# A fused attention and mixture-of-experts kernel on one core: first loads of the second stage issued some slots sooner, and four more weight pieces converted in its first pass

## The chip, the cores and the metric

The kernel runs on one core of a Trainium2 chip. The core has five engines that run programs of their own and wait for each other by semaphores: PE (TensorE, matmuls), DVE (VectorE), ACT (ScalarE), POOL (GpSimd) and SP (SyncE, here the queue that issues most DMAs; ACT issues a few). The time is device microseconds (us) of one execution; the kernel before has a median of 885.64 us over three.

## The reference

Three blocks stand behind each other. The weights `moe_w_in` and `moe_w_out` come as 8-byte floats, everything else as 4-byte ones.

```python
# 1: attention that mixes its heads before and after the softmax (4 x 12 heads x 448 x 64)
scores = scale * np.matmul(q, k.transpose(0, 1, 3, 2))
scores = np.einsum('bhij,hg->bgij', scores, w_pre)
attn = softmax(scores)
attn = np.einsum('bhij,hg->bgij', attn, w_post)
x = np.matmul(attn, v)                 # as 1792 tokens x 768
# 2: a gated layer, 768 -> 2048 -> 768
h = x @ w_in
x = (h - np.tanh(h)) @ w_out
# 3: 8 experts of 4 slots each
logits = x @ phi                       # 768 x 32
slot_input = softmax_over_tokens(logits).T @ x
slot_out[e] = np.maximum(slot_input[e] @ w1[e], 0) @ w2[e]
out = softmax_over_slots(logits) @ slot_out
```

## The kernel before

**Stage 1, attention (to about 437 us).** The work is cut into 184 *slots* (NS) of up to ten query rows times twelve heads. A slot passes over the engines in a pipeline that is written out by hand: PE scores, ACT copies them to `S`, SP regroups `S` to `D` by a DMA so that the heads lie side by side (`regroup`, L304, four slots ahead: D_AHEAD), PE mixes heads (`premix`, L313), DVE takes the maximum, ACT the exponential (`expo`, L325), PE mixes heads again (`postmix`, tile `tm`, L356), ACT copies that back (`gather`, L370 to L374), PE multiplies by v (`values`, `vx`, L395) and DVE copies the result to `xs` (L405). It goes to memory in four pieces `xd0` to `xd3`, one for each pass of stage 2. `postmix` and `gather` run four slots behind, so two slots' worth of them stand after the loop. Slots go in pairs.

Beside it, `Conversion` turns the 8-byte weights into 4-byte ones, in pieces of 128 x 384 values: SP loads 384 KB, ACT takes the absolute value (L50), DVE shifts exponents and joins head and tail in five instructions (L54, L55, L60, L65, L66), POOL adds (L71), SP stores 192 KB to `wi` or `wo`. There are 32 pieces of each matrix; a planner with an even rate gives each piece its slot.

**Stage 2 (to about 780 us)** goes over the tokens in four passes of 512, 512, 512 and 256, each in 16 steps `t` of 128 columns of w_in. A step multiplies x by its columns (`product`, PE, L840, 36 matmuls) and applies the gate h - tanh(h): `gate_act` (four ACT instructions, L860 to L867), `gate_first` (DVE L871, L872, L879) and `gate_last` (DVE L884, L885). The products are exact to fp32 by splitting both operands in two parts: `split_w` (ACT L787, then DVE or POOL L788), `split_x` (ACT L823, DVE L824). In the first pass the split weights are also saved to memory (`save_w`, a DMA that ACT issues, L801) and loaded from there in later passes. In that pass w_out is multiplied by phi (`turn_w`, PE `wt` L964 with copies by DVE L970 and ACT L968; `fold`, PE; copy to `wphi`, DVE L986), so that later `logits` (PE `lgp`, L995) needs it.

The last pieces of w_out, those of rows f = 12 to 15 (`LATE`), 8 pieces, are not converted in stage 1 but in the first pass: one a step from t = 4 to t = 11 (`late_load` two steps before, `late_first` at the step, `late_last` one step after, the store two after), and remain on chip in the buffer `ex[3]`. `save_w`, `late_load` and the loads of w_in share DMA queues with everything else.

**Between the stages.** Stage 2 is a generator (`more`), whose pieces the loop over slots calls. Its first piece issues the loads of the first four w_in units and of x; it stands at slot NS - 4, since its buffers take the place of stage 1's early pools. The other pieces stand between the last `postmix` and `gather`.

**Stage 3 (780 us to the end)** runs the experts, whose 4-byte weights arrive by DMA into buffers that stage 2 gives back one by one.

## Time and profile before

| | us |
|---|---|
| median of three runs (lowest, highest) | 885.64 (884.59, 890.2) |
| the profiled execution | 886.23 |
| its span in the profile | 884.5 |
| PE busy | 807.9 (91%) |
| ACT busy | 570.5 (64%) |
| DVE busy | 556.7 (63%) |
| POOL busy | 247.7 (28%) |

The profiled execution takes 1.73 us more than its span, which lies around the program. A row of a timeline gives the start, the duration, and in brackets how long the engine was idle before it and what released it. "SPq" and "ACTq" are DMAs being issued by those engines. Records of one engine overlap a little, because an instruction starts in the shadow of the one before. "issue" is time in which the engine waited for nothing that the profile shows.

### The profile page before, as it was taken

The numbers are of one execution on the slowest core, as the hardware profiler recorded it, in microseconds if no ns is written. First come the engines' busy times: TensorE is split into PE (matmuls) and PEld (weight loads), VectorE is DVE, ScalarE is ACT, GpSimd is POOL, SyncE is SP. The second block draws the span as 40 slices with busy tenths as digits, with TensorE's granted clock in tenths as the row PEclk, the third lists the DMA queues.
The fourth block names the chain that finished last, engine by engine and source line by source line (L and its number), as shares of the span: only waits on it lengthen the run. The fifth ranks groups of instructions, "written<-read, shape, count | busy, mean of one in ns | idle before, by whom it ended". The sixth has DMA issues, their size and how long they took to land.

```text
span 884.5 us, 28648 instructions
## 1 busy us (share of the span) xinstructions
PE 807.9 (91%) x11790; PEld 570.8 (65%) x11790; DVE 556.7 (63%) x1181; ACT 570.5 (64%) x1345; POOL 247.7 (28%) x428
## 2 busy tenths in 40 slices
PE   8889988799987999899899999999999999999965
PEld 6556665566665667566676667667776786964322
DVE  5357766577666777788456986566765777830104
ACT  4777887687776878798666776546664666821103
POOL 5234344334334444454303452000000003700000
PEclk9999999899999999999999999999999999999988
DMA  9787888768888788785759976678764457899998
GB/s 182 191 234 220 213 236 248 218 190 211 231 253 226 219 206 239 236 254 177 256 176 363 374 260 223 207 316 317 302 215 175 149 179 256 313 359 413 424 392 303
DMA packets 131766, 224.53 MB, mean 254 GB/s; under 512 B 44852, under 2 KB 112436, under 8 KB 128052
## 3 DMA queue, kind: packets, MB, share of 16 engines
q1 hardware_dynamic: 128288, 209.84, 74.8%
q10 hardware_dynamic: 3348, 12.87, 3.7%
q8 instruction: 93, 1.52, 0.7%
q14 instruction: 37, 0.30, 0.1%
HBM read 147.96 MB, written 36.18 MB: 208 GB/s over the span
## 4 chain that ended last, share of the span: by engine, by line
PE 50%; DMA 18%; ACT 13%; DVE 12%; issue 5%; SPq 1%; POOL 1%; ACTq 0%; POOLq 0%; DVEq 0%
PE hp L840 21%; DMA D<-S 7%; DMA ex<-in_moe_w_dram 7%; ACT e L325 6%; PE pm L313 5%; PE sc L279 5%; DVE mx L317 4%; PE vx L395 3%; PE tm L356 3%; PE gt L911 2%; ACT S L287 2%; PE kx L236 2%; PE lgp L995 2%; PE sp L1077 1%; ACT aT L370 1%
## 5 line engine op out<-in xcount | busy, mean ns | idle before, releaser
L325 ACT ACTIVATE e<-pm,mx 128x448 f32<-128x448 f32 x184 | 115.1, 631 | 86.3 <-DVE mx L317 84.9
L840 PE MATMUL hp<-xa,rg 128*128 128x512 f32 x576 | 152.7, 405 | 0.2 <-POOL rg L788 0.2
L317 DVE TENSOR_REDUCE mx<-pm 128x1 f32<-128x448 f32 x184 | 106.1, 618 | 73.5 <-PE pm L313 73.4
L356 PEld LDWEIGHTS tm<-wk,e 64*56 64x56 f32 x5888 | 104.7, 128 | 62.8 <-issue 32.4
L356 PE MATMUL tm<-wk,e 64*56 64x60 f32 x5888 | 113.5, 216 | 13.3 <-issue 7.9
L313 PE MATMUL pm<-D,wpre 64*64 64x448 f32 (+2 forms) x736 | 107.6, 565 | 18.4 <-DMA D<-S 15.2
L840 PEld LDWEIGHTS hp<-xa,rg 128*128 128x128 f32 x576 | 102.3, 188 | 28.9 <-issue 10.5
L287 ACT ACTIVATE S<-sc 120x448 f32<-120x448 f32 (+1 forms) x186 | 91.4, 553 | 4.6 <-PE sc L279 3.0
L279 PE MATMUL sc<-khi,qT 64*120 64x448 f32 (+1 forms) x384 | 83.6, 392 | 9.3 <-DVE xs L405 6.2
L342 POOL TENSOR_SCALAR wk<-wpost,rv 128x60 f32<-128x60 f32 x184 | 86.9, 503 | 16.5 <-DVE rv L335 13.8
L331 POOL TENSOR_SCALAR rv<-ss 128x2 f32<-128x2 f32 x92 | 24.5, 266 | 225.3 <-ACT e L325 194.6
L395 PE MATMUL vx<-aT,vn 128*64 128x120 f32 (+1 forms) x1536 | 83.9, 262 | 2.0 <-ACT S L287 1.3
L797 POOL TENSOR_TENSOR rg<-rg 128x384 fp32r<-128x384 f32 x24 | 23.9, 1012 | 208.8 <-DVE rg L794 205.0
L395 PEld LDWEIGHTS vx<-aT,vn 128*64 128x64 f32 x1536 | 74.7, 137 | 7.2 <-issue 3.0
L860 ACT ACTIVATE sq<-hp 128x512 f32<-128x512 f32 (+1 forms) x62 | 32.9, 530 | 68.0 <-PE hp L840 68.0
L370 ACT ACTIVATE aT<-tm 128x480 f32<-128x480 f32 x144 | 75.8, 593 | 0.1
L871 DVE SCALAR_TENSOR_TENSOR qd<-qd,sq 128x512 f32<-128x512 f32 (+1 forms) x61 | 37.6, 616 | 59.1 <-ACT mk L867 53.7
L840 PE MATMUL hp<-xb,rg 128*128 128x512 f32 x288 | 74.7, 404 | 0.0
L840 PEld LDWEIGHTS hp<-xb,rg 128*128 128x128 f32 x288 | 52.1, 188 | 16.6 <-issue 6.3
L279 PEld LDWEIGHTS sc<-khi,qT 64*120 64x120 f32 (+1 forms) x384 | 45.3, 173 | 26.1 <-PE tm L356 9.4
L71 POOL TENSOR_TENSOR fa<-fa,f 128x384 f32<-128x384 f32 x56 | 57.7, 1030 | 6.4 <-DVE f L66 2.1
L313 PEld LDWEIGHTS pm<-D,wpre 64*64 64x64 f32 (+2 forms) x736 | 23.9, 132 | 51.4 <-DMA D<-S 23.2
(199 smaller groups left out, 1391.3 us busy)
## 6 DMA issues: line engine op xcount, KB each, us to landing
ex<-in_moe_w_dram SPq DMA_DIRECT2D x21, 1536.0 KB
D<-S SPq DMA_DIRECT2D x144, 210.0 KB
rg<-wis SPq DMA_DIRECT2D x36, 768.0 KB
f<-in_moe_w_in_dram SPq DMA_DIRECT2D x32, 384.0 KB
wis<-rg ACTq DMA_DIRECT2D x16, 768.0 KB
f<-in_moe_w_out_dram SPq DMA_DIRECT2D x24, 384.0 KB
rg<-wi SPq DMA_DIRECT2D x19, 384.0 KB
wi<-fa SPq DMA_DIRECT2D x32, 192.0 KB
```

The source lines that it names most:

```text
L71: eng.tensor_tensor(out=out, in0=bits(a), in1=bits(p), op=ALU.add)
L279: nc.tensor.matmul(xs[e][0][:ni], lhsT=qT[n][s, l, p, :ni], rhs=kt[s], start=(i == 0), stop=(i == 2))
L287: nc.scalar.activation(out=dst, in_=xs[e][0][:ni], func=ACTF.Copy)
L313: nc.tensor.matmul(xs[x][64 * i:64 * i + 64], lhsT=wpre[k0:k1], rhs=d[i][k0:k1], start=True, stop=True)
L317: nc.vector.tensor_reduce(out=mx[:, x:x + 1], in_=xs[x], op=ALU.max, axis=AX.X, negate=True)
L325: nc.scalar.activation(out=es[x], in_=xs[x], func=ACTF.Exp, bias=mx[:, x:x + 1], accum_out=ss[:, x:x + 1])
L342: nc.gpsimd.tensor_scalar(out=wk, in0=wpost, scalar1=rv[:, x:x + 1], scalar2=None, op0=ALU.mult)
L356: nc.tensor.matmul(xs[i][64 * z:64 * z + JH, x, c], lhsT=es[x][h, j:j + JH], rhs=wks[x][h], start=True, stop=True)
L370: nc.scalar.activation(out=out[:, :, c0:c0 + m].rearrange("p a (x i) -> p a x i", x=2), in_=x, func=ACTF.Copy)
L395: nc.tensor.matmul(x[64 * e:64 * e + 64, i, :ni], lhsT=nat_v[b, h // NP][:, h % NP, c, :], rhs=a[:, c, h, :ni], start=(c == 0), stop=(c == ...
L840: nc.tensor.matmul(hp, lhsT=r32(w[:, m, hl, cs]), rhs=r32(x_of(b, c, l)), start=(c == 0 and i == 0), stop=(c == KD - 1 and i == 2))
L871: nc.vector.scalar_tensor_tensor(out=qd, in0=qd, scalar=TG_E, in1=sq, op0=ALU.add, op1=ALU.mult)
```

## The change

`LATE` goes from 12 to 10: 52 pieces, not 56, are converted in stage 1 and twelve in the first pass. `late_at` gives their steps: two at t = 4, two at t = 5, then one a step from 6 to 13. The raw buffers lie in `ex[4]` and half of `ex[5]`, the results stay in `ex[3]` and the first half of `ex[5]`; the two reloads of the rows 10 and 11 of w_out from memory are gone, the stores stay. Line numbers after the change are shifted: L787 is L816, L788 L817, L801 L830, L823 and L824 L850 and L851, L840 L867, L405 L415.

A pool `homes` holds three buffers through both stages. In stage 1, two of them serve as the landing place of k and as raw buffers of the conversion, and the third one is free. Stage 2 loads its first w_in and x into them. So the seven first loads are issued one at a time at the ends of the slots NS - 19, NS - 17, and so on to NS - 7.

The start of stage 2 is put in a different order: the first `split_w` and `split_x` stand at the ends of the last two slots, the first product is cut as 2 + 2 + 2 columns of x, and the second product, the third weight split and the first gate stand ahead of the last three `values`. Five warm-up matmuls on PE are removed.

```diff
-LATE = 12
+LATE = 10
...
+        if s == first_load:
+            more = follow()
+        if s >= first_load and (s - first_load) % 2 == 0 and s < first_load + 14:
+            next(more)
         if s == NS - D_AHEAD:
             early_stack.close()
-            more = follow()
+            next(more)
+        if s in (NS - 2, NS - 1):
             next(more)
...
+    for t in range(4):
+        load_first(t)
+        yield
+    xl = rgp.tile([128, XW], FP32, tag="xl", name="xa")
+    for a in range(0, KD, 2):
+        nc.sync.dma_start(
+            out=xl.rearrange("p (a s) -> p a s", a=KD)[:, a:a + 2], in_=xd[0][:, a:a + 2])
+        yield
...
+    late_at = {}
+    for i in range(len(late_w)):
+        late_at.setdefault(max(4 + i // 2, 2 + i), []).append(i)
...
-        if 0 <= t - 2 < len(late_w):
-            late_load(t - 2)
-        if 0 <= t - 4 < len(late_w):
-            on(3, f64_abs, nc, late_high(t - 4), late_raw(t - 4))
-            on(5, late_first, t - 4)
...
+        for i in late_at.get(t + 2, []):
+            late_load(i)
+        for i in late_at.get(t, []):
+            on(3, f64_abs, nc, late_high(i), late_raw(i))
+            on(5, late_first, i)
+        for i in late_at.get(t - 1, []):
+            on(5, late_last, i)
+        for i in late_at.get(t - 2, []):
+            on(5, late_store, i)
...
-    for t in range(4):
-        load_w(t)
-        if t == 0:
-            load_x(0)
     yield
     split_w(0, nc.vector)
     save_w(0)
-    idle = bank("h1", [128, 128], "warm")
-    for _ in range(5):
-        nc.tensor.matmul(idle, lhsT=ident, rhs=ident, start=True, stop=True)
-    for i in range(0, KD, 2):
-        for c in range(i, i + 2):
-            split_x(0, c)
-        yield
-        product(0, {}, i, i + 2)
+    split_x(0, 0)
+    yield
+    for c in range(1, KD // 2):
+        split_x(0, c)
+    yield
+    product(0, {}, 0, 2)
+    for c in range(KD // 2, KD):
+        split_x(0, c)
+    yield
+    product(0, {}, 2, 4)
+    yield
+    product(0, {}, 4, KD)
```

On SP, at the end of stage 1, before (`D<-S` are regroups, `rg<-wi` the units of w_in, `xa<-xd` pieces of x):

```order
L304 DMA D<-S 96x1x448 x2
L776 DMA rg<-wi_69 128x2x384
L819 DMA xa<-xd_65 128x1024 x3
L776 DMA rg<-wi_70 128x2x384
L776 DMA rg<-wi_71 128x2x384
L776 DMA rg<-wi_72 128x2x384
L380 DMA xd_68<-xs 768x1x120
L776 DMA rg<-wi_73 128x2x384
```

and after, the last part of the same stretch:

```order
L711 DMA rg<-wi_71 128x2x384
L314 DMA D<-S 108x1x448
L127 DMA wi_83<-fa 128x384
L314 DMA D<-S 108x1x448
L711 DMA rg<-wi_72 128x2x384
L314 DMA D<-S 108x1x448
L127 DMA wi_84<-fa 128x384
L314 DMA D<-S 108x1x448
L718 DMA xa<-xd_65 128x1024
L314 DMA D<-S 108x1x448
L127 DMA wi_84<-fa 128x384
L314 DMA D<-S 108x1x448
```

The loads of x and w_in moved from behind the last regroup to places between regroups and stores of the conversion.

On ACT, from the last pair of exponentials on, before:

```order
L325 ACTIVATE e,ss<-pm,mx 128x448 x2
L373 ACTIVATE aT<-tm 128x48x5
L374 ACTIVATE aT<-tm 128x48x4
L373 ACTIVATE aT<-tm 128x48x5
L374 ACTIVATE aT<-tm 128x48x4
L787 ACTIVATE rg<-rg 128x2x384
L801 DMA wis_89<-rg 128x1536
L823 ACTIVATE xa<-xa 128x512 x2
L373 ACTIVATE aT<-tm 128x48x5
```

and after:

```order
L335 ACTIVATE e,ss<-pm,mx 128x448 x2
L816 ACTIVATE rg<-rg 128x2x384
L830 DMA wis_89<-rg 128x1536
L850 ACTIVATE xa<-xa 128x512
L383 ACTIVATE aT<-tm 128x48x5
L384 ACTIVATE aT<-tm 128x48x4
L383 ACTIVATE aT<-tm 128x48x5
L384 ACTIVATE aT<-tm 128x48x4
L850 ACTIVATE xa<-xa 128x512 x5
```

The weight split L816, its save L830 and one split of x moved from behind the four copies of `gather` to ahead of them.

On DVE, from the last weight split ahead of the first gate on, before (`xs<-vx` are the copies of the last `values`):

```order
L788 TENSOR_TENSOR rg<-rg 128x2x384
L405 COPY xs<-vx 128x2x8x9
L405 COPY xs<-vx 128x2x2x8
L405 COPY xs<-vx 128x2x8x9
L405 COPY xs<-vx 128x2x2x8
L405 COPY xs<-vx 128x2x8x9
L405 COPY xs<-vx 128x2x2x8
L788 TENSOR_TENSOR rg<-rg 128x2x384
L871 SCALAR_TENSOR_TENSOR quad<-quad 128x512
L872 SCALAR_TENSOR_TENSOR quad<-quad 128x512
L879 TENSOR_TENSOR g_8453<-hp,g_8453 128x512
L884 SCALAR_TENSOR_TENSOR hp<-quad,hp 128x512
```

and after:

```order
L817 TENSOR_TENSOR rg<-rg 128x2x384 x2
L898 SCALAR_TENSOR_TENSOR quad<-quad 128x512
L899 SCALAR_TENSOR_TENSOR quad<-quad 128x512
L906 TENSOR_TENSOR g_8326<-hp,g_8326 128x512
L911 SCALAR_TENSOR_TENSOR hp<-quad,hp 128x512
L912 COPY_PREDICATED g_8326<-quad,hp 128x512
L415 COPY xs<-vx 128x2x8x9
L415 COPY xs<-vx 128x2x2x8
L415 COPY xs<-vx 128x2x8x9
L415 COPY xs<-vx 128x2x2x8
L415 COPY xs<-vx 128x2x8x9
L415 COPY xs<-vx 128x2x2x8
```

The first gate (L871 to L885, now L898 to L912) moved from behind the six copies of `values` to ahead of them.

On DVE, in the step t = 5 of the first pass, before:

```order
L871 SCALAR_TENSOR_TENSOR qd<-qd,sq 128x512
L872 SCALAR_TENSOR_TENSOR qd<-sq,qd 128x512
L879 TENSOR_TENSOR g<-hp,g 128x512
L884 SCALAR_TENSOR_TENSOR hp<-qd,hp 128x512
L885 COPY_PREDICATED g<-mk,hp 128x512
L54 TENSOR_SCALAR ex<-ex 128x384
L55 TENSOR_SCALAR ex<-ex 128x384
L60 SCALAR_TENSOR_TENSOR ex<-ex 128x384
L65 TENSOR_SCALAR ex<-ex 128x384
L66 SCALAR_TENSOR_TENSOR ex<-ex 128x384
L986 COPY wphi<-wq 128x128
L970 COPY ex<-wt 128x3x128
```

and after, from behind the gate on:

```order
L54 TENSOR_SCALAR ex<-ex 128x384
L55 TENSOR_SCALAR ex<-ex 128x384
L60 SCALAR_TENSOR_TENSOR ex<-ex 128x384
L54 TENSOR_SCALAR ex<-ex 128x384
L55 TENSOR_SCALAR ex<-ex 128x384
L60 SCALAR_TENSOR_TENSOR ex<-ex 128x384
L65 TENSOR_SCALAR ex<-ex 128x384
L66 SCALAR_TENSOR_TENSOR ex<-ex 128x384
L65 TENSOR_SCALAR ex<-ex 128x384
L66 SCALAR_TENSOR_TENSOR ex<-ex 128x384
L1018 COPY wphi<-wq 128x128
L1002 COPY ex<-wt 128x3x128
```

Of the conversion, two first halves (L54, L55, L60) and two second halves (L65, L66) stand now ahead of the copy to `wphi`, where one of each stood.

## Rows read from the trace of the kernel before

**Rows 1.** Windows: busy us of PE, PEld, DVE, ACT, POOL; PE clock, DMA share, GB/s

```profile
437.00:460.00 23.00, 19.48 (x291) 15.96 (x288) 13.42 (x25) 13.65 (x30) 1.01 (x3) 1.00 0.61 199
460.00:552.00 92.00, 86.47 (x474) 63.19 (x473) 71.07 (x126) 62.88 (x113) 39.38 (x27) 1.00 0.85 306
...
780.00:885.00 105.00, 83.43 (x704) 38.97 (x700) 18.64 (x49) 17.15 (x37) 2.31 (x8) 0.94 0.96 379
```

**Rows 2.** Waits of PE in stage 1: total us, times, longest

```profile
PE pm L313 <- DMA D<-S: 14.4, 9, 3.9
```

**Rows 3.** Timeline of PE where the stages meet

```profile
441.30 0.36 PE L356 MATMUL tm<-wk,e 64*56 64x60 f32 x9 [2.51 <-issue]
441.60 1.38 PE L1197 MATMUL warm<-ident 128*128 128x128 f32 x10
...
444.30 1.07 PE L356 MATMUL tm<-wk,e 64*56 64x60 f32 x64
...
448.26 3.86 PE L395 MATMUL vx<-aT,vn 128*64 128x88 f32 x96
452.06 5.73 PE L840 MATMUL hp<-xa,rg 128*128 128x512 f32 x24
458.54 0.66 PE L911 MATMUL gt<-ident,g 128*128 128x128 f32 x4 [0.76 <-DVE g L885]
```

**Rows 4.** Timeline of ACT in the same stretch

```profile
437.43 0.37 ACT L374 ACTIVATE aT<-tm 128x192 f32<-128x192 f32 x1
437.65 0.86 ACT L787 ACTIVATE rg<-rg 128x768 fp32r<-128x768 f32 x1
...
440.08 1.15 ACT L823 ACTIVATE xa<-xa 128x512 fp32r<-128x512 f32 x2 [1.57 <-DMA rg<-wi]
...
448.71 0.60 ACT L860 ACTIVATE quad<-hp 128x512 f32<-128x512 f32 x1 [1.53 <-PE hp L840]
...
450.44 0.71 ACT L867 ACTIVATE quad<-quad,tlimit 128x512 f32<-128x512 f32 x1
```

**Rows 5.** Timeline of DVE in the same stretch

```profile
449.75 0.48 DVE L405 COPY xs<-vx 128x144 f32<-128x144 f32 x2 [1.58 <-PE vx L395]
...
454.24 0.96 DVE L788 TENSOR_TENSOR rg<-rg 128x768 fp32r<-128x768 f32 x1 [1.58 <-ACT rg L787]
...
457.76 0.73 DVE L885 COPY_PREDICATED g<-quad,hp 128x512 f32<-128x512 int32 x1
```

**Rows 6.** Timeline of POOL in the same stretch

```profile
460.45 1.84 POOL L788 TENSOR_TENSOR rg<-rg 128x768 fp32r<-128x768 f32 x1 [22.08 <-ACT rg L787]
```

**Rows 7.** Timeline of DVE in the first pass

```profile
477.67 0.69 DVE L871 SCALAR_TENSOR_TENSOR qd<-qd,sq 128x512 f32<-128x512 f32 x1 [0.98 <-ACT mk L867]
...
480.95 0.35 DVE L54 TENSOR_SCALAR ex<-ex 128x384 f32<-128x384 f32 x1
...
482.59 0.56 DVE L66 SCALAR_TENSOR_TENSOR ex<-ex 128x384 f32<-128x384 uint32 x1
483.07 0.28 DVE L986 COPY wphi<-wq 128x128 f32<-128x128 f32 x1
...
517.38 1.43 DVE L54 TENSOR_SCALAR ex<-ex 128x384 f32<-128x384 f32 x1
...
538.29 0.29 DVE L986 COPY wphi<-wq 128x128 f32<-128x128 f32 x1 [1.69 <-PE wq L984]
```

**Rows 8.** Timeline of POOL in the first pass

```profile
517.30 1.29 POOL L824 TENSOR_TENSOR xb<-xb 128x512 fp32r<-128x512 f32 x1 [3.29 <-ACT xb L823]
```

**Rows 9.** Waits of PE in the first pass

```profile
PE wt L964 <- DVE ex L970: 3.1, 4, 1.1
PE lgp L995 <- DVE wphi L986: 1.5, 3, 0.7
```

**Rows 10.** Windows: the first 40 us of the first pass

```profile
460.00:500.00 40.00, 37.29 (x205) 27.88 (x204) 30.14 (x56) 27.68 (x50) 14.36 (x10) 1.00 0.99 363
```

**Rows 11.** Waits of SP's queue in the first pass

```profile
SPq L776 <- DMA wis<-rg: 33.5, 9, 8.1
```

More of the change, by code (lines that the diff above doesn't have):

```diff
@@ L82, in __init__, with place @@
         self.t = {}
+        self.loads = 0
+    def place(self, x):
+        n = x.shape[1] // 4
+        self.raw = [x[:, i * n:(i + 1) * n] for i in range(4)]
+        self.raw += [self.pool.tile([128, n], FP32, tag="f64", name="f64", bufs=1)]
     def load(self, j):
         f, hf, o = j
-        r = self.pool.tile([128, self.CV, 2], I32, tag="f64", name="f64", bufs=self.bufs)
+        r = self.raw[self.loads % self.bufs].bitcast(I32).rearrange("p (f w) -> p f w", w=2)
+        self.loads += 1
         if o:
@@ L152, in talking_heads @@
     cv.pool = er
+    kns = box["homes"].tile([128, NP * 2 * NR * HD], FP32, tag="rgs", name="kn")
+    cv.place(box["homes"].tile([128, 4 * 2 * cv.CV], FP32, tag="xl", name="f64"))
     psq = early_stack.enter_context(tc.tile_pool(name="at_psq", bufs=2, space=PSUM))
@@ L161, in load_k @@
     def load_k(b, p):
[L162 removed]
+        n = 2 * NR * HD
+        t = kns[:JP, p * n:(p + 1) * n].rearrange("p (e r d) -> p e r d", e=2, r=NR)
         nc.sync.dma_start(out=t, in_=k[b, 2 * p:2 * p + 2].rearrange("e (p r) d -> p e r d", r=NR))
@@ L816, in load_x @@
         dst = dst.rearrange("p (a s) -> p a s", a=KD)
-        step = KD if p else 2
-        for a in range(0, KD, step):
-            nc.sync.dma_start(out=dst[:, a:a + step], in_=xd[p][:, a:a + step])
+        nc.sync.dma_start(out=dst, in_=xd[p])
     def split_x(b, c, eng=nc.vector):
@@ L1172, in step @@
             mem["slow"] = True
-            for l in range(2):
-                give(xap.tile([128, EXB], FP32, tag=f"x{l}", name="ex"))
+            give(xap.tile([128, EXB], FP32, tag="x0", name="ex"))
+            give(rgp.tile([128, EXB], FP32, tag="xl", name="ex"))
         if b == NPASS - 1:
@@ L1533, in fused_kernel @@
     }
+    box["homes"] = ctx.enter_context(tc.tile_pool(name="homes", bufs=1, reuse_waits="tile"))
     with tc.manual_schedule():
```

43 lines of the change are left out of this document (22 added, 21 removed).

## The prediction

> **What bounds the kernel now.** I read the stages first, as windows of time, and then the waits of the engine that is busiest in each. In the stretch where the stages meet, PE is busy 19.48 of 23 us while DMA moves 199 GB/s; in the first pass PE is busy 86.47 of 92 us, DVE 71.07; at the end DMA is at 0.96 of its time and PE is not the limit [rows 1]. So up to the last stage PE sets the pace, and what counts is where it waits. The last stage waits for weights, whose buffers stage 2 gives back at fixed steps; the change leaves those steps and their order alone, so I let the end move as much as the end of the first pass moves.
>
> The second view is PE's waits. In attention nine waits for the regroup's DMA make 14.4 us, the longest 3.9 [rows 2]. Where the stages meet, PE stands for 2.51 us ahead of the last matmuls of a `postmix`, with no releaser in the profile, then runs 1.38 us of warm-up matmuls, and later waits 0.76 us for the first gate [rows 3]. In the first pass its waits are small: 3.1 us in four for a copy of turned weights and 1.5 us in three for `wphi` [rows 9]. What the change could take away is thus about 14 us in attention and about 5 us where the stages meet; what it can add is DVE work in a pass where DVE is the second busiest engine.
>
> **Where the stages meet.** I follow the new order with the old durations, starting where both are alike, at the end of the last exponential. Before, `gather` comes next and ends at 437.80; the weight split of 0.86 us follows, and ACT then stands for 1.57 us [rows 4]. The row names a load as the releaser, but ACT's issue of the save stands in between, and this needs DVE's half of the split: its 0.96 us and an issue of about 0.6 make as much without any load. Now that chain stands ahead of `gather`: 0.86 + 1.57 and one split of x (half of 1.15, so 0.58) make 3.0 us, and `gather` ends at 440.8. The wait that used to delay only the splits of x now delays the copies that free the tile of the next `postmix`. PE: `postmix` of 1.07 us to 441.9, twelve matmuls of the first product at 5.73 / 24 = 0.239 us to 444.7, `postmix` to 445.8, six more to 447.2, and eighteen of the second product to 451.5 [rows 3]. ACT: the first gate's four instructions take 2.44 us from 448.71 to 451.15 [rows 4], so now from 447.2 to 449.7, `gather` to 450.7 (it took about 1.1 us), the third weight split to 451.5. DVE: its half of that split and the gate took 4.25 us, from 454.24 to 458.49 [rows 5], so now to 455.8. Behind the gate stand the copies of the last `values`, 0.48 us a group [rows 5]. PE has done two of the three groups by then (1.29 us each, a third of 3.86 [rows 3]), to 454.1, and stands 2.2 us for the third one's bank, which the first copy gives free at 456.3; it is through with that group at 457.6 and with six matmuls more at 459.0. So the turn of the first gate begins at 459.0 rather than 458.54 [rows 3], without a wait for the gate.
>
> What ends last is another chain: the copy of the third group to 458.1, the issue of its store on ACT (0.6, as above), the second gate's 2.44 to 461.1, the fourth weight split's 0.86 to 462.0, and POOL's half of it, 1.84, to 463.8. Before, POOL ended at 460.45 + 1.84 = 462.29 [rows 6]. That is **+1.6**. The removed work (2.51 + 1.38 + 0.76 = 4.7 us of PE [rows 3]) is spent on waits that the new order makes: 3.0 for `gather`, 2.2 for the copies. The low end is that the new waits all find cover: −4.7. The high end is that the wait of 2.51 turns up again: +4.1. That the first loads are issued earlier gains nothing more by itself: what it takes away is ACT's wait ahead of the splits of x, which is already in this chain.
>
> The wait of 2.51 us has no releaser in the rows, and it stands in the middle of a group of like matmuls, with DMA busy. The Trainium skill (Runtime: NRT & Kernel Launch, Instruction fetch mechanics) says that an engine's instructions come in blocks over a queue of the sequencer's own and that crossing a block is mostly hidden. If that rule held here, the wait would have another cause, which nothing in the change would take away, and the sum would be 2.5 us higher; the row shows a wait that is not hidden, and a burst of first loads stands right ahead of it, so I let it go with the burst and give the other case 0.2, inside the range of my forecast.
>
> **First pass.** Four more pieces are converted here. One clean piece takes DVE from 480.95 to 483.15, 2.20 us for five instructions [rows 7], about 1.3 for the three ahead of the step's end and 0.9 for the two of the next step (by their number). Steps 4 and 5 get a piece more each. Step 4 has 1.3 more, of which the 0.98 us idle ahead of the next gate hides most [rows 7]; 0.3 is left. In step 5 the copy to `wphi` at 483.07 stands right behind the conversion, without idle time [rows 7]; 1.3 + 0.9 = 2.2 more come ahead of it, and the logits wait for that copy already [rows 9]. Together 2.4. Step 6 gets a second half of 0.9 more after a step that ran late: 0.3. Before, the conversion ended with step 12; now step 12 has a first half more (1.3 against some 0.98 of idle, 0.35) and step 13 a whole piece (2.2 against 1.69 us idle ahead of its `wphi` copy at 538.29 [rows 7], 0.5, and 0.25 ahead of the gate). Sum **+3.8**. The two reloads that go are of no use to PE, which waits for no DMA in this pass. Low end +1 (idle time takes in all but step 5's half); high end four whole pieces, 8.8, and one instruction of the kind next paragraph tells of, 1.1: +9.9.
>
> One of the shifts took 1.43 us at 517.38 instead of 0.35, while POOL ran its split of x from 517.30 for 1.29 us [rows 7, 8]. The Trainium skill (SBUF — State Buffer, Who interferes with whom) names the reason: DVE and GpSimd share a pair of ports as an exclusive lock, so that the loser stands for a whole instruction. The trace agrees, and it speaks against more DVE work beside POOL's; if all four extra pieces met it, the pass would cost 4 x 1.1 = 4.3 us more than the sum has.
>
> **Attention.** Four pieces of 56 fewer are loaded, converted and stored. PE, not the conversion, sets the time of a pair of slots, so the instructions that go are hidden and worth nothing. What can shrink are the waits for regroups: a share of 4/56 of 14.4 is 1.0; all of them would be 14.4; with the conversions dealt out anew and seven loads set among the last regroups, one more of the longest, +3.9, can come [rows 2]. The nine waits have a mean of 1.6; I take two fewer, **−3**, nearer to the share than to the whole, because the waits come singly and a lower rate moves them more than it removes them.
>
> **Sum.** +1.6 + 3.8 − 3 = +2.4 on the profiled execution's 886.23 is 888.6. That execution was 0.6 above the median of 885.64, so the forecast is 888.0 us.
>
> **Rivals.** *The waits go.* If most of the waits for regroups are due to the rate of conversion and the new start finds cover, −10 − 4.7 + 3.8 gives −11: 875. For it: the waits are the largest loss of PE in attention. Against it: nine waits over 180 slots look like chance meetings in the queues, and the ACT order puts a wait ahead of `gather`. Chance 0.10.
>
> *The first pass becomes bound by its queue (slower).* In its first 40 us DMA is at 0.99 and 363 GB/s [rows 10], and SP's queue waits 33.5 us in nine waits for saves before it may issue a load of w_in [rows 11]. The four extra pieces bring 4 x 384 KB of loads and 4 x 192 KB of stores, less 2 x 384 KB of reloads: 1536 KB, at 363 GB/s 4.3 us. Most of it falls on steps 2 to 5, where two late pieces a step stand among the loads of w_in. If those loads land after the step that splits them, PE waits 4.3 us, and the conversions that come in a heap behind it find no idle time (8.8): 4.3 + 8.8 + 1.6 − 3 = +11.7, 897. It decides when a load of w_in lands later than ACT is free to split it. Against it: PE now waits for none of these loads [rows 9]. Chance 0.15.
>
> *Attention doesn't care.* The waits stay as they are, and only costs are left: +1.6 + 3.8 = +5.4, 891. For it: single waits, not a steady lack. Chance 0.25. My own forecast has 0.50.
>
> **How the numbers follow.** A measurement of this kernel tells a change of about 1% (8.9 us: 876.8 and 894.5) from none. Faster by more is the first rival alone, 0.10; slower by more is the second, 0.15; the rest is 0.75. The range runs from 878 (attention at −8 with the start at −3 and the pass at +3.8) to 897 (the second rival's sum); it leaves out the first rival and what may lie beyond the second, together under 0.2.
>
> **What would show it.** Right: ACT's wait for the save ahead of `gather`, near 437 to 440; PE standing two us between the second and third group of the last `values`; no long wait of PE in the middle of `postmix`; longer waits of `lgp` for `wphi` in the first pass, and PE's time from the first turn of a gate to the end of that pass 3 to 5 us longer. Wrong: the waits of `pm` for regroups well under 8 us or over 18; PE waiting for splits of w_in in the first pass; the last stage taking up a shift rather than passing it on.

## The result: 1.1% slower, outside the forecast range

The changed kernel takes 898.84 us (median of four), the one before 887.92 over four executions beside it (885.64 over the three that the forecast started from): a ratio of 1.0111 with an interval of 1.0069 to 1.0152, so 6 to 13 us more. The forecast was 888.0, with 878 to 897 as its range. The ratio on 885.64 would give 895.5, so the range is missed narrowly; the three terms of the sum are missed by more.

The profiled execution of the changed kernel has a span of 895.3 us, 10.8 more than before. Four marks show where they went. The last exponential of attention ends at 437.29 (436.79 before). POOL's first split of weights, with which I ended the sum of the start, ends at 465.82 (462.29 before [rows 6]). The second pass's first matmul starts at 562.04 (551.13), and the last product of stage 2 starts at 786.95 (774.82). So attention costs +0.5, the place where the stages meet **+3.0**, the first pass **+7.4**, the other passes +1.2, and stage 3 takes 1.3 back. The windows of the changed kernel say the same, beside [rows 1]: PE is busy for less time than before in both of these stretches, and DVE for more in the second, the first pass.

```profile
437.00:460.00 23.00, 17.83 (x279) 14.79 (x276) 11.53 (x22) 11.04 (x27) 1.06 (x3) 0.93 0.51 183
460.00:552.00 92.00, 80.25 (x427) 57.05 (x426) 74.58 (x134) 62.24 (x110) 42.19 (x30) 0.98 0.84 284
```

**Where the stages meet.** The two waits that the new order makes are there as forecast: 2.99 us ahead of a `postmix` for `gather` (3.0 in the sum) and 2.18 us for the copy that stands behind the first gate (2.2 in the sum). Rows of PE:

```profile
440.76 2.22 PE L366 MATMUL tm<-wk,e 64*56 64x60 f32 x64 [2.99 <-ACT aT L384]
442.91 3.63 PE L867 MATMUL hp<-xa,rg 128*128 128x512 f32 x12
...
458.03 1.43 PE L405 MATMUL vx<-aT,vn 128*64 128x88 f32 x32 [2.18 <-DVE xs L415]
...
465.87 0.73 PE L867 MATMUL hp<-xa,rg 128*128 128x512 f32 x2 [1.37 <-POOL rg L817]
```

On ACT the row of the first split of x shows what `gather` stood behind: the split of 0.84 us, the save, and 1.42 us until DVE was done:

```profile
437.18 0.84 ACT L816 ACTIVATE rg<-rg 128x768 fp32r<-128x768 f32 x1
439.04 0.35 ACTq L830 DMA_DIRECT2D wis<-rg  x1
439.43 0.63 ACT L850 ACTIVATE xa<-xa 128x512 fp32r<-128x512 f32 x1 [1.42 <-DVE rg L817]
```

What the sum did not have is in the same rows of PE: 64 matmuls of `postmix` take 2.22 us, not 1.07 [rows 3], and twelve of the product 3.63, not 2.87. The granted clock of that stretch is 0.60; it was 1.00 while PE ran before the wait and in the part of the wait up to 440. So part of the window runs at half clock, the lower of the two levels (1.2 instead of 2.4 GHz). These two groups take 1.9 us more than the sum had; about 1.4 of that is the clock, since with the clock up the same two take 1.42 and 3.04 us (section 3 of the experiments). Windows of 4 us, with the granted clock third from the end:

```profile
436.00:440.00 4.00, 1.77 (x32) 1.54 (x32) 1.83 (x3) 2.58 (x7) 0.22 (x1) 1.00 0.05 22
440.00:444.00 4.00, 3.24 (x67) 2.86 (x68) 3.16 (x7) 4.00 (x12) 0.84 (x2) 0.60 0.44 179
444.00:448.00 4.00, 4.00 (x77) 3.17 (x76) 2.08 (x3) 1.38 (x4) 0.00 (x0) 0.97 0.51 177
```

**First pass.** The stretch from the end of step 4 to the end of step 5 makes 6 of the 7.4 us. Rows of DVE, then of POOL: one L60 takes 2.06 us, the others 0.56, while POOL splits weights from 480.19 for 1.92 us; one L66 takes 1.25 instead of 0.56 while POOL adds; and the copy to `wphi` (L1018) comes only behind all of them.

```profile
480.46 2.06 DVE L60 SCALAR_TENSOR_TENSOR ex<-ex 128x384 int32<-128x384 int32 x1
...
489.93 1.25 DVE L66 SCALAR_TENSOR_TENSOR ex<-ex 128x384 f32<-128x384 uint32 x1
491.11 0.28 DVE L1018 COPY wphi<-wq 128x128 f32<-128x128 f32 x1
```

```profile
480.19 1.92 POOL L817 TENSOR_TENSOR rg<-rg 128x768 fp32r<-128x768 f32 x1 [4.70 <-PE gt L938]
489.76 1.01 POOL L71 TENSOR_TENSOR ex<-ex 128x384 f32<-128x384 f32 x1 [7.66 <-issue]
```

PE pays for both: 2.16 us for the turned weights behind the long L60, and 2.82 us for `wphi`, where the longest such wait of before was 0.7 [rows 9].

```profile
483.05 0.55 PE L996 MATMUL wt<-ident,ex 128*128 128x128 f32 x3 [2.16 <-DVE ex L1002]
...
491.44 0.62 PE L1027 MATMUL lgp<-g,wphi 128*32 128x512 f32 x1 [2.82 <-DVE wphi L1018]
...
492.82 1.65 PE L867 MATMUL hp<-xa,rg 128*128 128x512 f32 x3
```

Behind the second wait the clock is granted at 0.62, and the three matmuls of the product at 492.82 take 1.65 us instead of 0.96. The windows of the changed kernel come first, then the rows of the kernel before at the place of the two waits' ends (no wait ahead of the turned weights, 0.96 for the product):

```profile
487.00:491.00 4.00, 1.62 (x11) 1.22 (x10) 3.86 (x8) 3.56 (x6) 1.01 (x1) 1.00 0.55 105
491.00:495.00 4.00, 3.56 (x15) 1.94 (x16) 0.39 (x2) 0.00 (x0) 2.78 (x2) 0.62 0.97 383
```

```profile
477.19 0.49 PE L964 MATMUL wt<-ident,ex 128*128 128x128 f32 x3
...
484.40 0.96 PE L840 MATMUL hp<-xa,rg 128*128 128x512 f32 x3
```

**Attention.** Between 20 and 437 us, PE's waits for regroups went from 15.2 us (14.4 of them in [rows 2], which starts at 45) to 8.4, but its waits with no releaser went from 6.1 to 11.7, and attention is no shorter. At the first exponential of slot 176 the changed kernel is 3.1 us ahead (421.9 against 425.0); the last eight slots give that back. Two of its waits:

```profile
PE pm L323 <- DMA D<-S: 8.4, 9, 2.9
...
PE vx L405 <- issue: 4.2, 4, 1.8
```

### The profile page after: what moved, and what is told of

The parts are those of the page before. It is cut to its first block, busy times and chain, and to the rows that moved or that the text cites. A ratio compares the mean times of both kernels' runs of the same rounds, so it can differ in the third digit from the quotient of the medians.

```text
span 895.3 us, 28609 instructions
## 1 busy us (share of the span) xinstructions
PE 813.2 (91%) x11780; PEld 574.3 (64%) x11780; DVE 557.2 (62%) x1181; ACT 570.2 (64%) x1345; POOL 246.5 (28%) x428
## 3 DMA queue, kind: packets, MB, share of 16 engines
q8 instruction: 93, 1.52, 0.7%
## 4 chain that ended last, share of the span: by engine, by line
PE 51%; DMA 16%; DVE 15%; ACT 10%; issue 6%; POOL 1%; SPq 0%; ACTq 0%; POOLq 0%; DVEq 0%
PE hp L867 20%; DMA D<-S 8%; DMA ex<-in_moe_w_dram 6%; PE pm L323 6%; PE sc L289 5%; ACT e L335 4%; PE vx L405 4%; DVE mx L327 4%; PE tm L366 3%; ACT S L297 2%; PE gt L938 2%; PE kx L246 2%; PE lgp L1027 2%; PE sp L1109 1%; DMA f<-in_moe_w_in_dram 1%
## 5 line engine op out<-in xcount | busy, mean ns | idle before, releaser
L867 PE MATMUL hp<-xa,rg 128*128 128x512 f32 x576 | 155.2, 409 | 1.4 <-POOL rg L817 1.4
L366 PEld LDWEIGHTS tm<-wk,e 64*56 64x56 f32 x5888 | 106.5, 130 | 62.2 <-issue 37.0
L867 PEld LDWEIGHTS hp<-xa,rg 128*128 128x128 f32 x576 | 103.4, 191 | 31.4 <-issue 10.9
L405 PE MATMUL vx<-aT,vn 128*64 128x120 f32 (+1 forms) x1536 | 85.9, 264 | 7.3 <-issue 4.2
L405 PEld LDWEIGHTS vx<-aT,vn 128*64 128x64 f32 x1536 | 75.7, 138 | 13.4 <-issue 9.8
L867 PE MATMUL hp<-xb,rg 128*128 128x512 f32 x288 | 75.1, 406 | 0.0
L898 DVE SCALAR_TENSOR_TENSOR qd<-qd,sq 128x512 f32<-128x512 f32 (+1 forms) x61 | 37.5, 615 | 56.0 <-ACT mk L894 50.6
L867 PEld LDWEIGHTS hp<-xb,rg 128*128 128x128 f32 x288 | 52.1, 189 | 16.9 <-issue 6.4
L71 POOL TENSOR_TENSOR fa<-fa,f 128x384 f32<-128x384 f32 x52 | 53.5, 1030 | 8.3 <-DVE rv L345 3.2
```

The costliest lines, as they stand in the source:

```text
L71: eng.tensor_tensor(out=out, in0=bits(a), in1=bits(p), op=ALU.add)
L366: nc.tensor.matmul(xs[i][64 * z:64 * z + JH, x, c], lhsT=es[x][h, j:j + JH], rhs=wks[x][h], start=True, stop=True)
L405: nc.tensor.matmul(x[64 * e:64 * e + 64, i, :ni], lhsT=nat_v[b, h // NP][:, h % NP, c, :], rhs=a[:, c, h, :ni], start=(c == 0), stop=(c == ...
L867: nc.tensor.matmul(hp, lhsT=r32(w[:, m, hl, cs]), rhs=r32(x_of(b, c, l)), start=(c == 0 and i == 0), stop=(c == KD - 1 and i == 2))
L898: nc.vector.scalar_tensor_tensor(out=qd, in0=qd, scalar=TG_E, in1=sq, op0=ALU.add, op1=ALU.mult)
```

## Experiments

Each kernel has one profiled execution, and in attention these differ by several us (the last exponential ends between 434.3 and 445.2 us in the kernels below). What comes behind differs less between kernels that have the same code there: by up to 1.5 us in the place where the stages meet, by up to 1.4 in the first pass. So the table has the ratio of the timed executions to the kernel before, the end of the last exponential, the time from there to the end of the span, and the last eight slots (from the start of the first exponential of slot 176 to the end of the last one).

| kernel | ratio (interval) | last exponential ends | from there to the end | last eight slots |
|---|---|---|---|---|
| before | 1 | 436.8 | 447.7 | 11.8 |
| after | 1.0111 (1.0069 to 1.0152) | 437.3 | 458.0 | 15.4 |
| new start, LATE 12 | 1.0071 (1.0040 to 1.0102) | 440.0 | 452.9 | 14.8 |
| late pieces alone | 1.0058 (1.0023 to 1.0094) | 441.0 | 456.0 | 11.8 |
| early loads alone | 1.0011 (0.9982 to 1.0039) | 443.2 | 446.5 | 16.2 |
| after, late pieces one a step | 1.0096 (1.0067 to 1.0125) | 439.2 | 456.1 | 16.3 |
| new start, gather first | 1.0044 (1.0013 to 1.0075) | 439.8 | 450.2 | 16.1 |
| new start, values first | 1.0041 (1.0014 to 1.0069) | 437.4 | 450.0 | 16.7 |
| new start, warm-up | 1.0064 (1.0027 to 1.0101) | 443.3 | 449.8 | 14.8 |
| new start, values first and warm-up | 1.0036 (1.0008 to 1.0064) | 439.4 | 449.7 | 14.9 |
| new start, gather first and warm-up | 1.0100 (1.0060 to 1.0139) | 445.2 | 449.3 | 16.3 |
| after, warm-up | 1.0123 (1.0080 to 1.0166) | 444.8 | 456.3 | 16.0 |
| early loads of w_in alone | 0.9970 (0.9939 to 1.0000) | 434.3 | 446.8 | 11.8 |
| the same, with late pieces one a step | 1.0046 (1.0019 to 1.0073) | 435.9 | 450.6 | 11.8 |

**1. The parts by themselves.** The changed kernel with LATE at 12 (new start), the kernel before with the late pieces (late alone), and the first of these with the kernel before's start (early loads alone).

```diff
# new start, LATE 12: the changed kernel with
-LATE = 10
+LATE = 12
...
-        late_at.setdefault(max(4 + i // 2, 2 + i), []).append(i)
+        late_at.setdefault(4 + i, []).append(i)
```

> The changed kernel with LATE back at 12 and one late piece a step from t = 4: only the early loads and the new start of stage 2 are left. Theory A (the loss is in two places, 3 us where the stages meet and 7 to 8 us in the first pass): +2 to +4 us on the kernel before, of which PE's 3.0 us wait for gather and the half clock behind it are seen again; the first pass takes as long as before. Rival B (loads among the last regroups cost attention 4 to 5 us, since a lead of 5.9 us at slot 154 had shrunk to 1.1 at slot 178): +6 to +9 us, and the end of the last exponential comes 3 us or more later than before. Rival C (the whole loss is the first pass): 0 us or less.

Measured: 1.0071, about 6 us, which is rival B's figure and not theory A's 2 to 4. From the last exponential on it is 5.2 us longer than before, 4.3 of them where the stages meet, and the first pass is as before (the longest wait for `wphi` is 0.7 us again). The two long waits and the half clock are there again (a `postmix` of 2.22 us, a product of 3.70), and here the second wait lowered the clock too, so that 32 matmuls of `values` take 2.61 us and not 1.43:

```profile
443.49 2.22 PE L366 MATMUL tm<-wk,e 64*56 64x60 f32 x64 [3.00 <-ACT aT L384]
445.64 3.70 PE L867 MATMUL hp<-xa,rg 128*128 128x512 f32 x12
...
460.86 2.61 PE L405 MATMUL vx<-aT,vn 128*64 128x88 f32 x32 [2.15 <-DVE xs L415]
```

```diff
# late alone: the kernel before with LATE = 10 and late_at, as in the change
-LATE = 12
+LATE = 10
...
+        late_at.setdefault(max(4 + i // 2, 2 + i), []).append(i)
```

> The kernel before with LATE at 10 and the doubled late schedule, but its own loads and start of stage 2. Theory A: +5 to +8 us, with the long wait of lgp for wphi (2 to 3 us) and one of wt for its copy (2 us) in steps 4 and 5 of the first pass. Rival B: 0 to +3 us, the first pass's loss given back by attention. If attention gains from four pieces fewer (my prediction's 3 us), the end of the last exponential is at about 434 and not 436.7.

Measured: 1.0058, about 5 us; 8.3 us more behind the last exponential, 6.7 of them in the first pass and 1.1 where the stages meet. The long L60 (2.05 us) and the wait of 2.2 us for the turned weights are there. The clock fell behind this wait already (granted 0.58 from 486 to 490), and the wait for `wphi` is 1.2 us, not 2 to 3. The last exponential of its profile ends at 441.0, not at 434, but a single one tells nothing there.

```diff
# early loads alone: as new start, LATE 12, with the kernel before's start
-        if s in (NS - 2, NS - 1):
-            next(more)
...
     split_w(0, nc.vector)
     save_w(0)
-    split_x(0, 0)
-    yield
...
+    idle = bank("h1", [128, 128], "warm")
+    for _ in range(5):
+        nc.tensor.matmul(idle, lhsT=ident, rhs=ident, start=True, stop=True)
+    for i in range(0, KD, 2):
+        for c in range(i, i + 2):
+            split_x(0, c)
+        yield
+        product(0, {}, i, i + 2)
```

> As the run with LATE at 12 and the early loads, but with the kernel before's order at the start of stage 2, its warm-up matmuls included. Theory A: 0 to -3 us: the burst of first loads at the end of attention is gone, with PE's wait of 2.5 us in the middle of a postmix, and nothing else changes. Rival B: +3 to +5 us, all of it between slots 154 and 184.

Measured: 1.0011, no change. Behind the last exponential it is 1.2 us shorter than before, as theory A had it; but its last eight slots take 16.2 us, not 11.8, as rival B had it for the end of attention. Each is right in its place, and the two cancel in the time. Rows of SP in this kernel: the first load of x (L716, 422.96) stood 2.7 us for the last conversion, whose buffers it takes; the stores of x (L392) wait for DVE; the third load of x stands behind them; and the last two regroups (L314) are issued only at 433.31, behind it. The stores stand ahead of the last two regroups in the kernel before too; the loads of x among them are what is new.

```profile
422.96 0.33 SPq L716 DMA_DIRECT2D xa<-xd  x1
...
428.99 3.53 SPq L392 DMA_DIRECT2D xd<-xs  x2
432.57 0.64 SPq L716 DMA_DIRECT2D xa<-xd  x1
433.31 1.60 SPq L314 DMA_DIRECT2D D<-S  x2
```

The wait of that first load, among the waits of SP:

```profile
SPq L716 <- POOL fa L71: 2.7, 1, 2.7
```

So the new start costs about 6 us between the first and the third of these kernels (452.9 against 446.5), the late pieces 5, and the early loads nothing in sum.

**2. The late pieces dealt evenly.**

```diff
-        late_at.setdefault(max(4 + i // 2, 2 + i), []).append(i)
+        late_at.setdefault(min(4 + i, 14), []).append(i)
```

> The changed kernel with its twelve late pieces dealt one a step from t = 4 (the last two together at t = 14), so that step 5 has one first half and one second half ahead of its copy to wphi as before. Theory A: 3 to 5 us less than the changed kernel, since the 2.8 us wait of lgp, the half clock behind it and the 2.2 us wait of wt go; some 1 us comes back at the end of the pass. A rival (four more pieces cost their DVE time wherever they stand): no more than 1 us less than the changed kernel.

Measured: 1.0096 against 1.0111, too near to tell apart by time. In the profile the first pass has neither the long wait for `wphi` nor the one of 2.2 us for the copy; a new one stands at its end.

```profile
PE wt L996 <- DVE ex L1002: 3.8, 5, 1.1
PE lgp L1027 <- DVE wphi L1018: 1.5, 3, 0.7
PE gt L938 <- DVE ex L1002: 1.5, 1, 1.5
```

From the last exponential on it is 1.9 us shorter than the changed kernel. That is less than the 3 to 5 expected. The first pass is 2.5 us longer than before instead of 7.4, and the two pieces at step 14 push another 1.1 into the second pass. The start, with the same code, lost 1.5 us more: the half clock behind the first wait lasted longer, and the twelve matmuls of the product take 5.05 us.

```profile
442.70 2.22 PE L366 MATMUL tm<-wk,e 64*56 64x60 f32 x64 [3.03 <-ACT aT L384]
444.85 5.05 PE L867 MATMUL hp<-xa,rg 128*128 128x512 f32 x12
```

**3. Inside the new start.** Three edits of the kernel with the new start and LATE 12, one at a time.

```diff
# gather first
-        if s in (NS - 2, NS - 1):
-            next(more)
+        if s == NS - 1:
+            next(more)
+            next(more)
```

> The run with the early loads and the new start alone (LATE 12), with the first weight split, its save and the first split of x put behind the first gather on ACT instead of ahead of it. If PE's 3.0 us wait for gather and the half clock of TensorE behind it (1.9 us of longer matmuls) come from that order: the postmix after the wait takes 1.1 and not 2.2 us, the wait is under 0.5 us, and from the end of the last exponential to the second late step it takes 2 to 4 us less. Rival (the splits of x are what the first product waits for, so that the wait only moves): PE waits 2 to 3 us at the first product, and nothing is gained.

Measured: 1.0044; 2.7 us less behind the last exponential. The wait for `gather` is gone (0.21), but PE now waits 1.72 us at the first product for a split of x, nearly what the rival had (2 to 3), and that product of twelve takes 4.75 us.

```profile
440.54 1.42 PE L366 MATMUL tm<-wk,e 64*56 64x60 f32 x64 [0.21 <-ACT aT L384]
443.68 4.75 PE L868 MATMUL hp<-xa,rg 128*128 128x512 f32 x12 [1.72 <-ACT xa L851]
```

```diff
# values first
-    gate_first(0)
-    gate_last(0)
     yield
+    gate_first(0)
+    gate_last(0)
     gate_act(1)
```

> The run with the early loads and the new start alone, with the first gate put behind the last values on DVE again. If the copies that stand behind the gate are what PE waits 2.2 us for: that wait goes, ACT issues the last store of x some 4 us earlier and the second gate follows, so 2 to 4 us less from the last exponential to the second late step. Rival (the wait is cover for the gate, which now waits instead): the wait moves to the turn of the first gate and the sum stays within 1 us.

Measured: 1.0041; 2.9 us less. The wait moved to the turn of the first gate with the same length, as the rival had it. Half of the 2.9 us is not this edit: behind the same wait of 3.00 us for `gather` the clock happened to stay at 1.00 here, and from the end of that wait to the second `postmix` it takes 4.33 us, not 5.78. Behind the second wait the clock did fall (granted 0.57 from 460 to 464), and fifteen matmuls take 5.29 us.

```profile
440.90 1.42 PE L366 MATMUL tm<-wk,e 64*56 64x60 f32 x64 [3.00 <-ACT aT L384]
442.25 3.04 PE L867 MATMUL hp<-xa,rg 128*128 128x512 f32 x12
...
459.63 0.73 PE L938 MATMUL gt<-ident,g 128*128 128x128 f32 x4 [2.21 <-DVE g L912]
460.04 5.29 PE L867 MATMUL hp<-xa,rg 128*128 128x512 f32 x15
```

```diff
# warm-up in the wait
     yield
+    idle = bank("h1", [128, 128], "warm")
+    for _ in range(10):
+        nc.tensor.matmul(idle, lhsT=ident, rhs=ident, start=True, stop=True)
     for c in range(1, KD // 2):
         split_x(0, c)
```

> The run with the early loads and the new start alone, with ten warm-up matmuls on PE in its 3.0 us wait for gather. If the granted clock fell because PE stood, the postmix behind the wait takes 1.1 and not 2.2 us and twelve matmuls of the first product 2.9 and not 3.7: 1.5 to 2 us less there, with the wait's end unchanged. Rival (something else slows PE there, such as ACT and DVE working on its operands): both stay long.

Measured: 1.0064, and 3.1 us less behind the last exponential. The wait ends where it did, but the `postmix` behind it takes 1.42 us instead of 2.22 and the twelve matmuls 3.04 instead of 3.70. (The ten warm-up matmuls make twenty records.)

```profile
443.69 2.50 PE L1227 MATMUL warm<-ident 128*128 128x128 f32 x20
446.77 1.42 PE L366 MATMUL tm<-wk,e 64*56 64x60 f32 x64 [0.57 <-ACT aT L384]
448.11 3.04 PE L867 MATMUL hp<-xa,rg 128*128 128x512 f32 x12
```

Since the clock can stay up without a warm-up too, three more kernels have the ten matmuls: values first, the changed kernel itself, and gather first (with seven, ahead of its first product).

> New start and LATE 12 with values ahead of the first gate, and ten warm-up matmuls in the wait for gather, so that the clock stays up as in the run with the warm-up alone. If values first gains by itself (the second gate no longer stands behind the copies): 2 us or more less behind the last exponential than the run with the warm-up alone, 447 to 448 us. If its gain was the clock only: 449 to 450.5 us, as with the warm-up alone.

> The changed kernel with ten warm-up matmuls in the wait for gather and nothing else. If the warm-up keeps the clock up: twelve matmuls of the first product take 3.0 us (3.6 to 5.1 without), and from the last exponential to the end it takes 455.5 to 456.5 us instead of 458.0; in time 1 to 3 us less than the changed kernel, a ratio of 1.008 to 1.010. If the clock falls by chance in any case: 3.6 us or more for the product, 458.

> New start and LATE 12 with gather first, and seven warm-up matmuls ahead of the first product, where PE waited 1.7 us for a split of x and the product then took 4.75 us. If that product was long for the clock: 3.0 to 3.2 us, and 448 to 449 us behind the last exponential instead of 450.2. If it waits within for splits of x: about 4.7 again.

Measured: with the clock up behind the first wait, the order of values is worth nothing (449.7 against 449.8), and gather first 0.5 (449.3). But behind the second wait the clock fell with values first (granted 0.71 from 460 to 464; fifteen matmuls take 4.97 us, against 4.15 with the loads of x last, below) and not with the warm-up alone, so that some 1 us of gain by that order is not ruled out. In the changed kernel the warm-up does what it should behind the first wait (3.06 for the product) and the sum behind the last exponential falls from 458.0 to 456.3, but here the second wait of 2.2 us lowered the clock, and the time is the changed kernel's within the interval (1.0123 against 1.0111). With gather first the product takes 3.46 instead of 4.75, short of the 3.0 to 3.2 expected.

```profile
449.65 3.06 PE L867 MATMUL hp<-xa,rg 128*128 128x512 f32 x12
...
464.23 1.43 PE L405 MATMUL vx<-aT,vn 128*64 128x88 f32 x32 [2.15 <-DVE xs L415]
465.60 2.93 PE L867 MATMUL hp<-xa,rg 128*128 128x512 f32 x6
```

```profile
449.02 3.46 PE L868 MATMUL hp<-xa,rg 128*128 128x512 f32 x12
```

So in all three with a warm-up in the wait for `gather` the product behind it takes 3.0 to 3.1 us. Without it, that is 3.6 to 5.1 in five kernels and 3.04 in one (those of section 5 counted in). What the new order costs with the clock up is 449.3 to 449.8 against the 446.5 of early loads alone, 3 us; the clock adds up to 3 more.

The time of the whole kernel shows no gain by the warm-up in any of the four pairs: 1.0064 with it against 1.0071 without, 1.0036 against 1.0041, 1.0123 against 1.0111, and with gather first even 1.0100 against 1.0044. What the clock costs is thus read from the profiles alone, one a kernel.

**4. The loads of x behind the last regroup.**

```diff
# early loads alone, with
         nc.sync.dma_start(
             out=xl.rearrange("p (a s) -> p a s", a=KD)[:, a:a + 2], in_=xd[0][:, a:a + 2])
-        yield
...
-        if s >= first_load and (s - first_load) % 2 == 0 and s < first_load + 14:
+        if s >= first_load and (s - first_load) % 2 == 0 and s < first_load + 8:
             next(more)
```

> The run with early loads and the kernel before's start, with the three loads of x put behind the last regroup again, so that only the four loads of w_in are early. If the loads of x delay the last regroups (by standing on SP for the last conversion, and by their transfers): the last eight slots, from slot 176's exponential to the end of the last one, take 11.8 us as in the kernel before and not 16.2, and the time is 2 to 5 us less than with all loads early, so 0 to -3 us on the kernel before. Rival (the w_in loads ahead of them do it, or the spread of attention from one execution to the next): still 14 us or more.

Measured: 0.9970 (0.9939 to 1.0000), some 3 us less than before, with an interval that just reaches no change: the fastest of all these kernels. Its last eight slots take 11.8 us again, and PE's wait of 2.51 us in a `postmix` does not come back, though the three loads of x still go as one burst. The rows of SP: the last two regroups (L314, at 424.83) are issued ahead of the loads of x, which are first used some 10 us later. Which of the three loads of x delayed the regroups is not shown, as all three were moved. The four early loads of w_in are not free there either: from slot 166's exponential to slot 176's it takes 20.9 us, 18.7 in the kernel before.

```profile
423.46 1.28 SPq L392 DMA_DIRECT2D xd<-xs  x2
424.83 1.58 SPq L314 DMA_DIRECT2D D<-S  x2
426.46 2.63 SPq L716 DMA_DIRECT2D xa<-xd  x3
```

The last eight slots are the clearest number of this study: 11.8 us in the four kernels of the table without early loads of x, 14.8 to 16.7 in the ten with them.

**5. The long L60.** The changed kernel with one weight split of the first pass on DVE.

```diff
-... split_w(t + 1, nc.gpsimd))
+... split_w(t + 1, nc.vector if t == 4 else nc.gpsimd))
```

> The changed kernel with one weight split of the first pass, that of step t = 4, done by DVE instead of POOL. If the L60 of 2.06 us at 480.46 (0.56 elsewhere) stood because POOL's split ran from 480.19 to 482.11: it takes 0.56 here, and PE's wait of 2.2 us for the copy behind it falls by about 0.5 us, since DVE has 0.96 us of the split itself. Rival (L60 is long for another reason, its place behind five others or its operands): it takes about 2 us here as well, and the wait grows by 1 us.

Measured: the L60 is as long as before, but I had moved the wrong split, that of the step ahead; POOL's split still runs beside it.

```profile
481.36 2.05 DVE L60 SCALAR_TENSOR_TENSOR ex<-ex 128x384 int32<-128x384 int32 x1
```

```profile
481.09 1.91 POOL L817 TENSOR_TENSOR rg<-rg 128x768 fp32r<-128x768 f32 x1 [10.46 <-ACT rg L816]
```

The next kernel moves the split of step 5 (`t == 5`).

> The changed kernel with the weight split of step t = 5, not 4, done by DVE instead of POOL: in the run before this one the split that POOL ran beside the long L60 (481.09 to 483.00) was that of step 5, so the wrong one was moved. If the long L60 stands for POOL's split: it takes 0.56 us here, and PE's wait of 2.1 us for the copy behind it falls to about 0.6; DVE's own 0.96 comes later, ahead of the next gate. Rival (long for another reason): about 2 us again.

Measured: the L60 takes 0.56 us. DVE's own split of 0.95 stands ahead of the copy, not behind it as I had expected, so PE's wait falls from 2.16 to 1.52 only, and the first pass is still 7.0 us longer than before. So what is shown is why this L60 is long, and not that the pass gets shorter without POOL's split. (Both of these kernels, timed in two executions, are as slow as the changed kernel or slower: 1.0103, 1.0055 to 1.0150, and 1.0193, 1.0142 to 1.0245. Nothing rests on that.)

```profile
485.79 0.56 DVE L60 SCALAR_TENSOR_TENSOR ex<-ex 128x384 int32<-128x384 int32 x1
486.26 0.95 DVE L817 TENSOR_TENSOR rg<-rg 128x768 fp32r<-128x768 f32 x1
```

```profile
487.74 0.55 PE L996 MATMUL wt<-ident,ex 128*128 128x128 f32 x3 [1.52 <-DVE ex L1002]
```

**6. Is there a gain of four pieces fewer that the early loads hid?** The kernel of 4 with LATE at 10 and the late pieces one a step.

```diff
-LATE = 12
+LATE = 10
...
-        late_at.setdefault(4 + i, []).append(i)
+        late_at.setdefault(min(4 + i, 14), []).append(i)
```

> The run with only the w_in loads early and the kernel before's start, and in addition LATE at 10 with the late pieces one a step from t = 4. By the account of the runs so far: start -1.8 us, first pass +3.6 us (all of it in steps 13 to 16), attention 0 to -3 us from four pieces fewer; in sum -1 to +2 us on the kernel before, and 1 to 4 us more than the run without the four pieces. From the end of the last exponential to the end 449 to 450 us (446.8 without the four pieces, 447.7 before). Rival (four pieces fewer make attention 5 us shorter, which the early loads of x have hidden so far): 3 to 5 us less than the kernel before.

Measured: 1.0046 (1.0019 to 1.0073), slower than the kernel without the four pieces. Behind the last exponential it takes 450.6 us, 3.8 more than without. By the ratios it is 6.7 us slower than without them, so attention is not shorter for it; in its profile a single wait with no releaser takes 4.6 us. The rival falls.

The profiles of all sixteen kernels say more on this than one. Seven have the four pieces fewer in attention, nine have not. Means of PE's waits between 20 and 437 us, with the range in brackets:

| | seven with four pieces fewer | nine with all |
|---|---|---|
| waits for regroups | 10.2 (7.7 to 13.3) | 13.8 (10.4 to 16.7) |
| waits with no releaser | 12.9 (8.5 to 17.6) | 7.7 (5.0 to 15.5) |
| all waits that the view lists | 39.7 (37.2 to 44.3) | 39.6 (36.9 to 43.4) |
| start of slot 164's exponential, ahead of all early loads | 401.5 (399.0 to 406.7) | 400.8 (396.7 to 405.3) |

With four pieces fewer the waits for regroups are 3.6 us less, and waits with no releaser take their place: PE waits as long as before. What those waits are is not shown here, and the kernels differ in other edits too.

## Why the prediction was wrong

The three terms were +1.6, +3.8 and −3. They came out as +3.0 (4.3 to 4.5 in the four other kernels with this start as it is), +7.4 (6.0 to 7.0 in the four others that have the late pieces two a step) and +0.5.

**Where the stages meet: the chain was right, and its price was too low.** The waits of 3.0 and 2.2 us came within 0.05 us of the sum. "PE: `postmix` of 1.07 us" and 0.239 us a matmul behind a wait of 3 us is the step that failed: these are durations at the full clock, and the clock was 0.60 there. With the clock up the sum was right: in the two kernels with this order and the warm-up, POOL's first split ends 27.15 and 27.23 us behind the last exponential, and 25.51 in the kernel before, so +1.6 and +1.7. Without it, that is 28.5 in the changed kernel and 29.8 to 30.0 in the four others. The one kernel in which the clock stayed up without a warm-up shows that the fall is likely, not certain. The edits of the order alone then show why no single one of the two waits was worth much: taken away, each left another in its place (1.72 us for a split of x, 2.2 for the gate). The warm-up matmuls that the change removes were counted as 1.38 us won; in the kernel before they stand where PE has nothing to do. My other reasoning about this place holds: the wait of 2.51 us in a `postmix` with no releaser is there in the two kernels that have the old loads (2.5 and 2.1 us), and none of over 0.4 us stands in this stretch in the fourteen with early loads, so the case in which it returns did not come.

**First pass: the sum had the work but not its neighbours.** Of the 7.4 us, 2.2 are the wait behind the long L60, 2.1 the longer wait for `wphi` (my 2.4 for steps 4 and 5, which are 0.3 and 2.2 and so 2.5), 1.7 the clock behind that wait, 1.0 comes in step 13 (0.75 in the sum) and the rest in steps 6 to 8. The failing step is "Step 4 has 1.3 more, of which the 0.98 us idle ahead of the next gate hides most". With a second first half, DVE's L60 falls under POOL's split and stands for it: 2.06 − 0.56 = 1.5 us, shown by taking POOL's split away; behind it stands not only the gate but the copy of the turned weights, which PE then waits for. The L66 of 1.25 us beside POOL's add, 0.7 more ahead of `wphi`, is read from the rows and was not taken apart. I had told of this lock in a paragraph of its own, with a row of 1.43 us and a price of 4.3 us, and left it out of the sum. The Trainium skill (SBUF — State Buffer, Who interferes with whom) says that the order of issue decides which of the two engines is blocked. The trace agrees: the later one, DVE's L60, took 2.06 instead of 0.56 us, and POOL's split 1.92 against 1.85 before. The clock was the second thing that this sum left out, as it was in the first one.

**Attention: the waits for regroups shrank, and it was worth nothing.** "I take two fewer, **−3**" is the step that failed, and not by its size: over all profiles the waits for regroups are 3.6 us less with four pieces fewer, but as much waiting came elsewhere, and slot 164 comes no sooner (section 6). The sum took every wait that goes as time won. In the two profiles that the result compares they fell by 6.8 us, part of it by chance, as they range over 6 us among the nine kernels with all pieces. The other half of that step, "seven loads set among the last regroups, one more of the longest, +3.9, can come", could be read. It came every time, 3 to 5 us, in all ten kernels of the table with early loads of x, and in none without. I had it as an end of the range only, though SP's order, with the loads of x ahead of the last regroups, was there to be read.

Of the signs that I had named, the waits on ACT and PE came as told; PE's time from the first turn of a gate to the end of the first pass grew by 8.6 us, not 3 to 5.

Of the rivals, the first pass "bound by its queue" gave nearly the right time (897) for a wrong reason: PE waited for no load of w_in. *Attention doesn't care* was right about attention up to its last slots, and wrong about the two costs. The rule of the Trainium skill that I had weighed (Runtime: NRT & Kernel Launch, Instruction fetch mechanics) did not decide anything: the wait of 2.51 us went with the old loads, and what the other waits with no releaser are is not shown here.

## What to carry to other kernels

Put a price on every new wait of PE of some 3 us that is not only its length: here the matmuls behind it ran at half clock in five of six kernels and took 1.4 to 2.8 us more than with the clock up. In the profiles, ten matmuls without use in the wait took that away; in the times of the whole kernel it did not show. An earlier load is not free because its data is needed later: read what its queue holds behind it (here the last two regroups of attention), and move only those loads that have room; the four loads of w_in early and the three of x late were 0.3% faster than the kernel before (at the edge of the noise), where all seven early gave nothing. A wait that goes is time won only if no other takes its place: the waits for regroups shrank and PE waited as long. When DVE work is added beside GpSimd work, lay the two timelines over each other and count the instructions that would begin under a GpSimd one.

## What was not expected of the hardware

A DVE instruction of 0.56 us (two inputs in SBUF) that began 0.27 us after a GpSimd one of 1.92 us ended 0.41 us after it, at 2.06 us, so that most of its 0.56 us lay behind it; a TENSOR_SCALAR can also be hit (1.43 instead of 0.35 [rows 7, 8]). And the same wait costs different times in kernels that have the same code there. Behind the wait of 3.0 us, the twelve matmuls took 3.63 us in the changed kernel, 5.05 with the late pieces one a step and 3.04 with values first; behind the wait of 2.2 us, 32 matmuls took 1.43 us in the changed kernel and 2.61 with the new start alone. In all, the clock fell within 1.5 us of the end of this second wait in seven of the eleven kernels that have it. So a kernel with two such waits has times up to 3 us apart behind them, whatever else is edited, and an edit there is read in several executions or with the clock held up.
